# Rounding the angles of the tables in one VectorE step, own space for the first projection, and a new written-out order, in an attention and spectral-gate kernel on one core

## The chip, the cores and the metric

One core of one Trainium2 chip runs the whole program. The metric is the device time of one execution in microseconds, the lower the better; the time of the kernel before is the median of three runs.

## The reference, cut to what matters

There are 8 batches, 8 heads, 576 positions and 64 dimensions of a head. The first half is an attention with feature maps, the second a gate with a convolution over the sequence, done by Fourier tables.

```python
def phi(x):
    proj = np.einsum('bhsd,df->bhsf', x, w_phi)             # 64 -> 128 features
    proj = proj - np.max(np.abs(proj), axis=-1, keepdims=True)
    return np.concatenate([np.exp(proj), np.exp(-proj)], axis=-1)
q_p, k_p = phi(q), phi(k)
kv = np.einsum('bhsf,bhsd->bhfd', k_p, v)
z = np.sum(k_p, axis=2)
num = np.einsum('bhsf,bhfd->bhsd', q_p, kv)
den = np.einsum('bhsf,bhf->bhs', q_p, z)[..., None] + 1e-06
x = num / den                                               # then as [batch, 576, 512]
x1, x2, x3 = split(x @ w_proj)                              # 512 -> 3 * 512
x2_conv = irfft(rfft(x2, axis=1) * rfft(filter_fft, axis=0), axis=1)
out = (x1 * x2_conv * x3) @ w_out
```

All inputs and the output are float32; the matmuls take bf16.

## The kernel before

**Order.** The whole program is one list of words, `PLAN` (lines 26 to 184). `run` (L995 on) takes the words from first to last and calls the method of that name with the arguments behind it; `@n` is the PSUM bank that the word uses, and `ACT`, `DVE` or `POOL` the engine that does a copy or an elementwise step. Each engine, and each DMA queue, therefore does its instructions in the order in which their words stand, and an instruction that waits holds up all that stands behind it on its engine. Waits between engines are set from the tiles that instructions read and write. Buffers are rings (`RING`): `kn`, `qn`, `vn`, `kT` and `qT` have two each, one for even and one for odd batches.

**Loads.** `load,n,b` (L560) brings batch `b` of q, k or v from HBM to SBUF as bf16, 576 KB written, on GpSimd's (POOL's) queue; `loadh` (L566) half a batch, 288 KB; `w_load,proj,i` (L550) a third of the projection weights, 512 KB; `w_load,out` (L553) the output weights. All of them are issued by POOL, in the order of the list and between POOL's own arithmetic.

**Transposes.** The features need q and k with dimensions along partitions. Batch 0 is transposed on TensorE (`pt`, L582) and copied out of PSUM (`pte`). The other batches go by DMA transposes on SyncE's (SP's) queue: `trh,n,b,X` (L572), one for heads 0 to 3 (X = 0) and one for heads 4 to 7 (X = 1), 288 KB each. SP also issues the filter loads (L481, L485), the transposes of the attention's output (`trx` L786, `trxt` L791) and the stores of the result (`st` L994).

**Attention, for each batch.** `Pk` (L601) and `Qn` (L608) multiply k and q with `w_phi`, four words each; `Pkt` and `Qnt` (L616) do the ninth block of positions of all heads at once, so each of these two needs both halves of the transposed batch. `maxk`, `maxq` and their `t` forms (L677) are the maxima of absolute values on VectorE (DVE), `ex` (L663) the exponentials on ScalarE (ACT), `vs` (L719) scales v on POOL, `KV` (L734) sums keys times values, `Pq` (L635, L641) is the projection of q with its maximum taken off, `NE` (L748) the numerator and denominator, `rc` (L762) and `xn` (L767) the division.

**Gate, for each batch.** `f1` (L816) and `f2` (L822) fold the positions by sums and differences, `F` (L828, L832) is the Fourier transform with the tables `D` and `Dt`, `X1`, `X2`, `X3` are the projections (L872 and L850; `X1t`, `X3t` L881 for the last 64 positions), `X1e` copies the first projection to the tile `x1s`, `tm` (L913) multiplies the third into it, `Y1` (L860) multiplies the spectrum with the filter's, `m3` (L864) adds two products, `I` (L925) is the inverse transform with the table `inv` (`J`, L963, for the last batch), `Ip` and `Im` (L932) give `cv`, `ym` (L973) multiplies by `x1s`, `O` (L984) is the output projection, `Oe` its copy out of PSUM, `st` the store.

**Tables, once at the start.** POOL writes rows of numbers (`gen_rows`), DVE makes columns of factors (`gen_cols`, L364 on). An angle in turns is row times column plus a phase: ACT computes it (`gen_turns`, L424 and L428) into the tile `turn`; DVE rounds it to a whole number by a cast to int32 (L437) and subtracts that (L438, `gen_angles`); ACT takes the sine (`gen_sin`). `H` (L511) and `H_ev` are the filter's own transform. What is needed at the start alone lies in a scratch pool; `late` closes it and puts `T0` to `T4`, `x1s`, `es`, `cv`, `yT` and `o` in its place, so their first writes wait for the last readers of the scratch tiles.

Of the kernel before, what the change touches and what calls it, by code (L numbers as in the profile page):

```python
# [32 lines left out]
pte,DVE,k,0,0,0@6 gen_sin,0 trh,q,1,0 maxq,0,3@4 gen_back pte,ACT,q,0,0,1@0 Pk,0,1@6 Pk,0,0@2
gen_sin,2 Qnt,0@0 load,q,2 maxk,0,0@2 Qn,0,0@4 gen_sin,4 load,v,1 maxqt,0@0 filt_fold,POOL,0
ex,k,p,0,1@6 maxq,0,0@4 D1m@0 D1e,DVE@0 pt,k,0,1,0@4 pt,k,0,1,1@5 gen_ends,POOL pte,DVE,k,0,1,0@4
Qn,0,1@0 pte,ACT,k,0,1,1@5 ex,k,m,0,0@2 gen_five,DVE H,0@5 load,k,2 gen_neg maxk,0,1@6
filt_fold,POOL,1 ex,k,p,0,0@2 maxq,0,1@0 ex,k,m,0,1@6 Pk,0,2@2 maxk,0,2@2 mhi,0 Pkt,0@0 Pk,0,3@6
H_ev,ACT,0@5 mlo,POOL,0 H,4@4 maxkt,0@0 ex,k,m,0,2@2 H,3@5 maxk,0,3@6 em,p,0,0 exkt,p,0@0
vs,POOL,p,0,0 trh,k,1,0 H_ev,DVE,3@5 ex,k,p,0,2@2 ex,k,m,0,3@6 trm,0@2 H,2@3 H_ev,DVE,4@4 em,m,0,0
H,1@5 trme,DVE,0@2 em,p,0,1 exkt,m,0@0 vs,POOL,m,0,0 H_ev,DVE,2@3 ex,k,p,0,3@6 Pqt,0@0 H_ev,DVE,1@5  # L40
late Pq,0,1@2 exqt,m,0@0 Qn,1,3@6 exqt,p,0@0 vs,POOL,p,0,1 ex,q,p,0,1@2 maxq,1,3@6 KV,0,0@0
ex,q,m,0,1@2 trh,k,1,1 Pq,0,2@4 KVe,DVE,0,0@0 Qn,1,2@6 em,m,0,1 load,q,3 ex,q,p,0,2@4 Qnt,1@2
maxq,1,2@6 Qn,1,0@0 vs,POOL,m,0,1 ex,q,m,0,2@4 maxq,1,0@0 Pq,0,0@6 Qn,1,1@4 ex,q,p,0,0@6 maxqt,1@2
NE,0,1@0 load,v,2 maxq,1,1@4 ex,q,m,0,0@6 KV,0,1@2 rc,0,1@0 mhi,1 xn,0,1@0 NE,0,0@4 mlo,POOL,1
KVe,ACT,0,1@2 trm,1@6 rc,0,0@4 ptx,0,1@0 trme,ACT,1@6 xn,0,0@4 NEt,0@2 ptxe,ACT,0,1@0 NE,0,2@6
f1,POOL,0,0,0 rct,0@2 ptx,0,0@4 xnt,0,0@2 Pq,0,3@0 ptxe,ACT,0,0@4 rc,0,2@6 xnt,0,1@2 xn,0,2@6
f1,POOL,0,0,1 ex,q,p,0,3@0 ptxt,0@2 trh,q,2,0 Pqt,1@4 ptxte,DVE,0@2 ptx,0,2@6 ex,q,m,0,3@0 Pk,1,1@2
f2,POOL,0,0,0 ptxe,DVE,0,2@6 X1t,0@7 trh,q,2,1 maxk,1,1@2 exqt,m,1@4 NE,0,3@0 f2,POOL,0,0,1
X1te,ACT,0@7 X3t,0@6 exqt,p,1@4 rc,0,3@0 ex,k,p,1,1@2 xn,0,3@0 load,k,3 Pkt,1@4 tmt,0@6 ptx,0,3@0
ex,k,m,1,1@2 f1,POOL,0,1,1 maxkt,1@4 F,0,1@6 ptxe,DVE,0,3@0 Fet,ACT,0,1@6 f1,POOL,0,1,0 Pk,1,0@2  # L50
Fe,ACT,0,1@6 Pk,1,3@0 maxk,1,0@2 exkt,p,1@4 X1,0,2@6 exkt,m,1@4 f2,POOL,0,1,1 ex,k,p,1,3@0 X1,0,1@7
trh,k,2,0 X1e,DVE,0,2@6 f2,POOL,0,1,0 ex,k,p,1,0@2 X1,0,3@4 maxk,1,3@0 trh,k,2,1 ex,k,m,1,0@2
X1,0,0@6 load,q,4 X1e,DVE,0,3@4 X3,0,3@5 em,p,1,0 X1e,DVE,0,1@7 ex,k,m,1,3@0 vs,POOL,p,1,0
X1e,DVE,0,0@6 F,0,3@2 em,m,1,0 trh,k,3,0 tm,0,3@5 X3,0,0@0 Fet,ACT,0,3@2 Fe,ACT,0,3@2 F,0,2@4
vs,POOL,m,1,0 tm,0,0@0 X3,0,1@3 Fet,ACT,0,2@4 Fe,ACT,0,2@4 F,0,0@0 tm,0,1@3 Qnt,2@4 Pk,1,2@6
Fet,ACT,0,0@0 load,k,4 Fe,ACT,0,0@0 maxqt,2@4 Pkt,2@2 trh,k,3,1 ex,k,m,1,2@6 maxkt,2@2 X2,0,0@0
ex,k,p,1,2@6 X2,0,4@4 Y1,0,0@0 exkt,m,2@2 X2,0,1@5 exkt,p,2@2 maxk,1,2@6 Qn,2,1@0 KV,1,0@2 Y1,0,4@4
em,m,1,1 em,p,1,1 vs,POOL,m,1,1 Pq,1,1@6 maxq,2,1@0 KVe,ACT,1,0@2 X3,0,2@4 ex,q,p,1,1@6 Y1,0,1@5
Qn,2,2@0 ex,q,m,1,1@6 Pq,1,2@2 vs,POOL,p,1,1 tm,0,2@4 X2,0,2@5 ex,q,m,1,2@2 maxq,2,2@0 Pk,2,1@6
ex,q,p,1,2@2 X2,0,3@4 Y1,0,2@5 load,k,5 ex,k,p,2,1@6 NE,1,1@0 m3,POOL,0,0 Y1,0,3@4 Pq,1,0@2  # L60
ex,k,m,2,1@6 trh,q,3,0 rc,1,1@0 ex,q,m,1,0@2 maxk,2,1@6 Qn,2,3@4 m3,POOL,0,1 ex,q,p,1,0@2 maxq,2,3@4
Qn,2,0@6 NE,1,0@2 maxq,2,0@6 Pq,1,3@4 load,v,3 ex,q,m,1,3@4 trh,q,3,1 rc,1,0@2 xn,1,1@0 I,0,0@6
ex,q,p,1,3@4 xn,1,0@2 I,0,1@0 f1,DVE,1,0,1 trx,1,0 Ie,0,0@6 KV,1,1@2 f1,POOL,1,0,0 Ie,0,1@0 Im,0,0@6
mhi,2 Ip,0,0@6 Im,0,1@0 Pk,2,2@4 ym,POOL,0,0 Pk,2,3@6 Ip,0,1@0 KVe,ACT,1,1@2 maxk,2,2@4 ex,k,p,2,3@6
NEt,1@2 ym,POOL,0,1 NE,1,2@0 ex,k,m,2,3@6 rct,1@2 xnt,1,0@2 rc,1,2@0 trx,1,1 mlo,POOL,2 xnt,1,1@2
ex,k,p,2,2@4 f2,DVE,1,0,0 load,q,5 NE,1,3@2 maxk,2,3@6 ex,k,m,2,2@4 trxt,1 f2,POOL,1,0,1 rc,1,3@2
# [983 lines left out]
```

## Time and profile before

| | |
|---|---|
| runs | 340.84, 340.9 and 342.14 us, median 340.9 |
| the profiled execution's own time | 341.41 us |
| its span, first to last instruction | 339.6 us |
| mean granted TensorE clock | 0.975 |
| TensorE (PE) busy | 283.2 us, 83% |
| VectorE (DVE) busy | 269.4 us, 79% |
| ScalarE (ACT) busy | 225.3 us, 66% |
| GpSimd (POOL) busy | 217.3 us, 64% |
| DMA moved | 39.98 MB, 118 GB/s on average |

The profile is of one execution. 1.8 us of its time lie outside its span. Busy shares are averages over the whole span: the start is unlike the middle, so stretches are read one by one. TensorE's clock is given as a share of 2.4 GHz: 1.00 is that level and 0.50 is 1.2 GHz. Names such as `kn_78` in the rows of the order are tiles: `kn_77` and `kn_78` are the two buffers of `kn`, for even and odd batches, `qn_75` and `qn_76` those of `qn`, `vn_79` and `vn_80` those of `vn`.

### The profile page before, as it was taken

The numbers are of one execution on the slowest core, as the hardware profiler recorded it, in microseconds if no ns is written. First come the engines' busy times: TensorE is split into PE (matmuls) and PEld (weight loads), VectorE is DVE, ScalarE is ACT, GpSimd is POOL, SyncE is SP. The second block draws the span as 40 slices with busy tenths as digits, with TensorE's granted clock in tenths as the row PEclk, the third lists the DMA queues.
The fourth block names the chain that finished last, engine by engine and source line by source line (L and its number), as shares of the span: only waits on it lengthen the run. The fifth ranks groups of instructions, "written<-read, shape, count | busy, mean of one in ns | idle before, by whom it ended". The sixth has DMA issues, their size and how long they took to land.

```text
span 339.6 us, 10233 instructions
## 1 busy us (share of the span) xinstructions
PE 283.2 (83%) x4289; PEld 202.8 (60%) x4289; DVE 269.4 (79%) x450; ACT 225.3 (66%) x376; POOL 217.3 (64%) x186
## 2 busy tenths in 40 slices
PE   0566785887698997897999898999999899989992
...
GB/s 122 247 194 181 200 168 188 163 173 119 145 145 181 120 86 64 223 75 146 105 94 196 106 70 128 137 5 141 126 70 2 28 135 7 36 71 131 26 0 154
DMA packets 72030, 39.98 MB, mean 118 GB/s; under 512 B 52336, under 2 KB 66800, under 8 KB 71984
## 3 DMA queue, kind: packets, MB, share of 16 engines
...
q14 instruction: 13, 0.11, 0.1%
HBM read 33.75 MB, written 9.44 MB: 127 GB/s over the span
## 4 chain that ended last, share of the span: by engine, by line
PE 53%; DMA 21%; DVE 9%; POOL 6%; issue 4%; ACT 4%; SPq 1%; ACTq 0%; DVEq 0%; POOLq 0%
PE ps L872 13%; DMA kT<-kn 10%; PE ps L850 9%; DMA kn<-in_k_dram 7%; PE ps L984 6%; PE ps L925 5%; PE ps L734 4%; DMA out_dram<-o 2%; PE ps L828 2%; PE ps L748 2%; PE ps L832 2%; PE ps L881 2%; DVE xn L767 2%; DVE cv L932 2%; DMA xT<-xn 2%
## 5 line engine op out<-in xcount | busy, mean ns | idle before, releaser
L872 PE MATMUL ps<-xT,wproj 128*128 128x256 bf16 x512 | 64.7, 276 | 2.5 <-DMA xT<-xn 1.7
L973 POOL TENSOR_TENSOR yT<-cv,x1s 128x576 bf16<-128x576 f32 x27 | 34.1, 1277 | 37.1 <-DVE x1s L913 16.9
L872 PEld LDWEIGHTS <-wproj 128*128 128x128 bf16 x512 | 48.6, 99 | 12.1 <-issue 3.3
L677 DVE TENSOR_REDUCE mk<-ps 128x8 f32<-128x1024 f32 (+1 forms) x40 | 44.0, 1109 | 8.8 <-PE ps L616 6.4
L677 DVE TENSOR_REDUCE mq<-ps 128x8 f32<-128x1024 f32 (+1 forms) x40 | 43.6, 1109 | 8.5 <-PE ps L608 5.8
L719 POOL TENSOR_TENSOR vp<-vn,vp 128x1152 bf16<-128x1152 bf16 x16 | 35.8, 2235 | 8.7 <-ACT vp L713 8.5
L663 ACT ACTIVATE Eqp<-ps 128x1024 bf16<-128x1024 f32 x32 | 32.3, 1032 | 10.4 <-PE ps L641 10.4
L663 ACT ACTIVATE Eqm<-ps 128x1024 bf16<-128x1024 f32 x32 | 32.4, 1031 | 6.9 <-PE ps L641 6.9
L663 ACT ACTIVATE Ekm<-ps 128x1024 bf16<-128x1024 f32 x32 | 32.8, 1031 | 5.9 <-PE ps L601 3.0
L663 ACT ACTIVATE Ekp<-ps 128x1024 bf16<-128x1024 f32 x32 | 32.7, 1030 | 5.2 <-PE ps L601 5.2
L864 POOL TENSOR_TENSOR T<-T,T 128x1024 bf16<-128x1024 bf16 x12 | 25.3, 2126 | 16.4 <-DVE T L860 16.4
L984 PE MATMUL ps<-wout,yT 128*128 128x512 bf16 x144 | 33.5, 379 | 2.5 <-DVE yT L967 0.8
L281 ACT COPY o<-ps 128x512 f32<-128x512 f32 x35 | 20.4, 589 | 22.5 <-PE ps L984 17.1
L719 POOL TENSOR_TENSOR vm<-vn,vm 128x1152 bf16<-128x1152 bf16 x14 | 30.1, 2152 | 7.3 <-ACT vm L713 7.3
L816 POOL TENSOR_TENSOR SD<-xn 128x512 bf16<-128x512 bf16 x26 | 29.7, 1161 | 5.2 <-DVE xn L767 5.1
L850 PE MATMUL ps<-wproj,XF 128*128 128x512 bf16 x128 | 31.5, 388 | 0.0
L925 PE MATMUL ps<-inv,T 128*128 128x288 bf16 x168 | 25.6, 295 | 3.7 <-POOL T L864 1.9
L932 DVE TENSOR_TENSOR cv<-es,ps 128x288 f32<-128x288 f32 x56 | 22.5, 446 | 6.5 <-ACT es L929 5.8
L822 POOL TENSOR_TENSOR xf<-SD 128x512 bf16<-128x512 bf16 x24 | 27.3, 1158 | 0.4
L913 DVE TENSOR_TENSOR x1s<-ps,x1s 128x512 bf16<-128x512 f32 x32 | 21.7, 685 | 3.0 <-PE ps L872 2.4
L984 PEld LDWEIGHTS <-yT 128*128 128x128 bf16 x144 | 13.4, 98 | 17.3 <-issue 1.4
L860 DVE TENSOR_TENSOR T<-ps,HTo 128x1024 bf16<-128x1024 f32 x16 | 19.3, 1218 | 4.6 <-PE ps L850 4.3
(174 smaller groups left out, 676.5 us busy)
## 6 DMA issues: line engine op xcount, KB each, us to landing
...
```

The costliest lines, as they stand in the source:

```text
L663: self.nc.scalar.activation(e, p, AF.Exp, bias=0.0, scale=1.0 if g == "p" else -1.0)
L677: self.nc.vector.tensor_reduce(out=out, in_=src, axis=AX.X, op=ALU.max, apply_absolute_value=True)
L719: self.eng(eng).tensor_tensor(out=t[:, :, :, 0:64], in0=self.at("vn", b)[:, 2 * X:2 * X + 2], in1=t[:, :, :, 64:65].to_broadcast([128, 2, ...
L816: self.eng(eng).tensor_tensor(out=o[:, :, 2 * i:2 * i + 2, :], in0=x[:, :, 0:2, :], in1=x[:, :, 2:4, :], op=ALU.subtract if i else ALU.add)
L822: self.eng(eng).tensor_tensor(out=o[:, :, 2 * i:2 * i + 2, :], in0=x[:, :, 0:4:2, :], in1=x[:, :, 1:4:2, :], op=ALU.subtract if i else ALU ...
L850: self.mm(self.pb(0), l, w[:, kt, 512:1024], start=(kt == 0), stop=(kt == 3))
L864: self.eng(eng).tensor_tensor(out=Y, in0=Y, in1=self.at(f"T{2 * e + 1}", b), op=ALU.add)
L872: self.mm(o[:, d], w[:, kt, f0 + 128 * m:f0 + 128 * m + 128], y[:, 1, ::-1, ::-1] if d else y[:, 0], start=(kt == 0), stop=(kt == 3))
L925: self.mm(self.pb(e, 0, 288), l, inv[:, 2 * e + i if i < 2 else 4 + e, :], start=(i == 0), stop=(i == 2))
L932: self.nc.vector.tensor_tensor(out=self.at("cv", 4 * b + m)[:, :, odd, :], in0=self.at("es", 4 * b + m).rearrange("p (x t) -> p x t", t=32 ...
L973: self.eng(eng).tensor_tensor(out=self.at("yT", b)[:, m, 0:SEQ], in0=self.at("cv", 4 * b + m).rearrange("p x h t -> p (x h t)"), in1=self. ...
L984: self.mm(self.pb(0), y[:, kt, 128 * c:128 * c + 128], w[:, kt, :], start=(kt == 0), stop=(kt == 3))
```

## The change

**Angles.** `gen_turns` is gone. DVE computes row times column plus phase straight into an int16 tile (a `tensor_scalar` whose result is rounded by the type of its output), and one `scalar_tensor_tensor` gives row times column minus that whole number. The phase is added as the bias of the sine on ACT; the sines are split accordingly (two for `D`, four for `Dt`, two and two for `inv[0:4]`, two as before for the last). `gen_cols` is cut in two words and `gen_rows` in two, and three pairs of iota instructions become one each.

**Space.** `x1s` moves from the tiles that follow the scratch pool to the ones that stand from the start.

**Order.** Every line of `PLAN` is new. Words change engine in a few places: 8 of the 36 copies `Oe` go from ACT to DVE, 11 of the 32 `X1e` from DVE to ACT, 6 `Fe` and 3 `Fet` from ACT to DVE, 4 `pte` from ACT to DVE, and 2 `vs`, 1 `ym` and 3 `m3` from DVE to POOL, 3 `f1` from POOL to DVE.

```diff
-TWO_PI = 2.0 * math.pi
+TWO_PI = 6.283185
 PLAN = """
-zeros gen_rows w_load,phi filt_load,2 w_phi loadh,q,0,0 filt_loadt gen_cols loadh,q,0,1 filt_load,0
-load,q,1 loadh,k,0,0 filt_load,1 w_load,proj,0 filt_fold,DVE,2 gen_turns,2 loadh,k,0,1 gen_turns,4
...
+w_load,phi filt_load,2 filt_load,0 filt_load,3 filt_loadt filt_load,1 loadh,k,0,0 gen_part
+loadh,k,0,1 gen_ident gen_rows,0 loadh,q,0,0 zeros pt,k,0,0,1@0 pte,ACT,k,0,0,1@0 gen_cols,0
...
     def alloc(self):
...
         R("XFt", [128, 4, 128], BF16)
+        R("x1s", [128, 4, SEQ], BF16)
     def late(self):
...
         R("T4", [128, 512], BF16)
-        R("x1s", [128, 4, SEQ], BF16)
...
-    def gen_turns(self, i):
...
-            for sine in range(2):
-                a.activation(t[:, :, sine, :], self.fr[:, :, sine, :], AF.Identity,
-                             bias=col(8 if sine else 23), scale=col(i))
...
-    def gen_angles(self, eng, i):
-        e, r = self.eng(eng), self.span(i)
-        t, w = self.turn[:, r, :], self.whole[:, r, :]
-        e.tensor_copy(w, t)
-        e.tensor_tensor(out=t, in0=t, in1=w, op=ALU.subtract)
+    def gen_angles(self, i):
...
+        def rest(k, a, b, x):
+            v.scalar_tensor_tensor(out=self.turn[:, a:b].rearrange("p a x -> p (a x)"), in0=x,
+                                   scalar=col(k), in1=self.whole[:, a:b].rearrange(
+                                       "p a x -> p (a x)"), op0=ALU.mult, op1=ALU.subtract)
+        if i in (0, 2):
+            w = self.whole[:, i:i + 2].rearrange("p o (s f) -> p o s f", s=2)
+            for sine in range(2):
+                v.tensor_scalar(out=w[:, :, sine, :], in0=self.fr[:, :, sine, :], scalar1=col(i),
+                                scalar2=0.0 if sine else 0.25, op0=ALU.mult, op1=ALU.add)
+            rest(i, i, i + 2, self.fr.rearrange("p o s f -> p (o s f)"))
+            return
+        for k in ((3, 4), (5, 6, 7))[i - 3]:
+            v.tensor_scalar(out=self.whole[:, 1 + k], in0=self.nr, scalar1=col(k),
+                            scalar2=col(8 + k), op0=ALU.mult, op1=ALU.add)
+            rest(k, 1 + k, 2 + k, self.nr)
     def gen_sin(self, i):
...
-            a.activation(self.at("D"), t, AF.Sin, **kw)
...
+        def sin(o, x, bias, scale=TWO_PI):
+            a.activation(o, x, AF.Sin, bias=bias, scale=scale)
...
-        self.whole = s.tile([128, 9, 288], I32, name="whole")
+        self.whole = s.tile([128, 9, 288], I16, name="whole")
```

**The loads on POOL's queue, at the start of the program.** Before, q and k of batch 0 come with q of batch 1 between them, and behind `kn_78` (k of batch 1) five more loads stand ahead of the first `vs` (`vp_104`):

```order
L566 DMA qn_75<-in_q_dram 128x2x576 x2
L560 DMA qn_76<-in_q_dram 128x4x576
...
L560 DMA vn_79<-in_v_dram 128x4x576
L560 DMA kn_78<-in_k_dram 128x4x576
L553 DMA wout_67<-in_moe_w_out_dram 128x4x512
L550 DMA wproj_66<-in_moe_w_proj_dram 128x4x512
...
L560 DMA qn_75<-in_q_dram 128x4x576
L560 DMA vn_80<-in_v_dram 128x4x576
...
L560 DMA kn_77<-in_k_dram 128x4x576
...
L719 TENSOR_TENSOR vp_104<-vn_79,vp_104 128x18x64
```

After the change the same place reads:

```order
L577 DMA qn_76<-in_q_dram 128x4x576
L567 DMA wproj_66<-in_moe_w_proj_dram 128x4x512
...
L577 DMA kn_78<-in_k_dram 128x4x576
L577 DMA kn_77<-in_k_dram 128x4x576
L510 TENSOR_TENSOR fe<-fl 128x1024 x2
L736 TENSOR_TENSOR vp_104<-vn_79,vp_104 128x18x64
L718 TENSOR_TENSOR mh_89<-mq_87,mh_89 128x2x18
L736 TENSOR_TENSOR vm_119<-vn_79,vm_119 128x18x64
L736 TENSOR_TENSOR vp_105<-vn_79,vp_105 128x18x64
L736 TENSOR_TENSOR vm_118<-vn_79,vm_118 128x18x64
L567 DMA wproj_66<-in_moe_w_proj_dram 128x4x512
L577 DMA qn_75<-in_q_dram 128x4x576
```

k of batches 1 and 2 are now the last loads for a while: the second third of the projection weights, q of batch 2, v of batch 1 and the output weights moved behind batch 0's four `vs`.

**The transposes on SP's queue.** Before, and after, the first ones behind the filter loads are:

```order
L572 DMA_TRANSPOSE qT_82<-qn_76 128x9x128 x2
L572 DMA_TRANSPOSE kT_84<-kn_78 128x9x128 x2
L572 DMA_TRANSPOSE qT_81<-qn_75 128x9x128 x2
L572 DMA_TRANSPOSE kT_83<-kn_77 128x9x128 x2
L572 DMA_TRANSPOSE kT_84<-kn_78 128x9x128 x2
```

```order
L589 DMA_TRANSPOSE qT_82<-qn_76 128x9x128 x2
L589 DMA_TRANSPOSE kT_84<-kn_78 128x9x128 x2
L589 DMA_TRANSPOSE kT_83<-kn_77 128x9x128 x2
L589 DMA_TRANSPOSE qT_81<-qn_75 128x9x128 x2
L589 DMA_TRANSPOSE kT_84<-kn_78 128x9x128 x2
```

Batch 1 keeps its place (q, then k); of batch 2, k goes ahead of q, and within a pair the second half of k now goes first.

**ACT, from its first instruction to the sines of the last tables.** In the change:

```order
L281 ACT_TABLE_LOAD
L281 COPY kT_83<-ps 128x512
L458 ACT_TABLE_LOAD
...
L680 ACT_TABLE_LOAD
L680 ACTIVATE Ekm_108<-ps 128x1024
...
L458 ACT_TABLE_LOAD
L458 ACTIVATE inv_70<-turn,cols_74 128x288 x4
...
L680 ACT_TABLE_LOAD
L680 ACTIVATE Ekm_110<-ps 128x1024
...
L458 ACT_TABLE_LOAD
L458 ACTIVATE inv_70<-turn,cols_74 128x288 x2
L680 ACT_TABLE_LOAD
```

Before there were three such loads, for the turns (L424), the sines (L452) and the exponentials (L663); now there are seven, since two groups of sines stand between exponentials.

## Rows read from the trace of the kernel before

**Rows 1.** The page: busy time, the span in 40 slices.
```profile
PE 283.2 (83%) x4289; PEld 202.8 (60%) x4289; DVE 269.4 (79%) x450; ACT 225.3 (66%) x376; POOL 217.3 (64%) x186
...
PE   0566785887698997897999898999999899989992
```

**Rows 2.** Windows: start:end, length, busy PE PEld DVE ACT POOL, clock, DMA, GB/s.
```profile
0.00:10.30 10.30, 1.30 (x11) 1.14 (x12) 3.82 (x40) 3.60 (x6) 9.56 (x27) 1.00 0.74 146
10.30:43.40 33.10, 21.12 (x343) 13.73 (x340) 31.68 (x48) 29.83 (x47) 23.05 (x24) 1.00 1.22 198
43.40:57.20 13.80, 9.00 (x174) 7.14 (x174) 7.63 (x17) 7.92 (x15) 6.90 (x8) 0.83 1.26 180
57.20:85.30 28.10, 23.21 (x312) 16.05 (x311) 21.10 (x25) 18.87 (x30) 18.95 (x13) 0.90 1.10 158
85.30:121.80 36.50, 31.61 (x527) 22.93 (x527) 30.29 (x47) 23.64 (x41) 18.73 (x15) 0.95 0.90 142
121.80:160.70 38.90, 33.52 (x526) 24.19 (x523) 34.58 (x51) 25.26 (x42) 27.21 (x20) 1.00 0.69 120
160.70:195.30 34.60, 32.47 (x523) 23.38 (x523) 29.20 (x45) 23.78 (x41) 28.46 (x21) 1.00 0.72 127
...
333.10:339.60 6.50, 0.00 (x0) 0.00 (x0) 0.00 (x0) 1.07 (x2) 0.00 (x0) 0.72 0.64 148
```

**Rows 3.** Chain of waits that ended last, 0 to 62 us: start, us, what.
```profile
9.41 22.56 DMA kn<-in_k_dram
31.98 1.75 SPq L572
33.78 20.71 DMA kT<-kn
```

**Rows 4.** PE's timeline: the two waits for transposed k of batches 1 and 2.
```profile
54.54 0.29 PE L616 MATMUL ps<-wphi,kT 64*128 64x128 bf16 x2 [3.46 <-DMA kT<-kn]
...
69.51 0.23 PE L616 MATMUL ps<-wphi,kT 64*128 64x128 bf16 x2 [2.36 <-DMA kT<-kn]
```

**Rows 5.** DVE's timeline: the last division of batch 0 ahead of X1.
```profile
49.94 0.69 DVE L767 TENSOR_TENSOR xn<-ps,r 128x512 bf16<-128x512 f32 x1
```

**Rows 6.** DMA queues (packets, MB, share): POOL's queue q0, 4 to 36 us.
```profile
q0 software_dynamic: 4599, 4.87, 92.2%
```

**Rows 7.** The same, SP's queue q1, 28 to 32, then 64 to 68 us.
```profile
q1 hardware_dynamic: 565, 0.14, 27.1%
...
q1 hardware_dynamic: 2589, 0.65, 125.9%
```

**Rows 8.** Timeline of all engines at the start: where ACT and DVE begin the tables.
```profile
6.68 1.28 ACT L424 ACT_TABLE_LOAD   x1 [6.68 <-DVE cols L416]
...
9.78 0.63 DVE L491 CAST f<-flt 64x512 bf16<-64x512 f32 x1 [2.80 <-DMA flt<-in_moe_filter_fft_dram]
...
10.34 0.43 DVE L437 CAST whole<-turn 128x576 int32<-128x576 f32 x1
```

**Rows 9.** Groups by line and form: the angles on ACT, and on DVE.
```profile
L428 ACT ACTIVATE turn<-nr,cols 128x288 f32<-128x288 f32 x5 | 2.8, 611 | 0.0
L424 ACT ACTIVATE turn<-fr,cols 128x288 f32<-128x288 f32 x4 | 2.3, 615 | 0.0
...
L438 DVE TENSOR_TENSOR turn<-turn,whole 128x576 f32<-128x576 f32 x3 | 2.3, 758 | 0.1
L437 DVE CAST whole<-turn 128x576 int32<-128x576 f32 x3 | 1.4, 467 | 0.0
```

**Rows 10.** ACT's timeline around its third table load.
```profile
19.76 0.95 ACT L456 ACTIVATE inv<-turn,cols 128x288 bf16<-128x288 f32 x2
20.73 1.28 ACT L663 ACT_TABLE_LOAD   x1
...
22.03 1.02 ACT L663 ACTIVATE Ekp<-ps 128x1024 bf16<-128x1024 f32 x1
```

**Rows 11.** Chain of waits, 150 to 170 us: start, us, what.
```profile
156.40 4.21 POOL T L864 x2
...
162.31 0.50 PE ps L748 x16
162.81 0.21 PE ps L635 x2
...
169.59 0.40 PE ps L608 x8
```

**Rows 12.** Groups by form: a maximum, and m3's sum on DVE.
```profile
L677 DVE TENSOR_REDUCE mq<-ps 128x8 f32<-128x1024 f32 x32 | 38.6, 1215 | 6.2 <-PE ps L608 5.8 <-ACT Ekm L663 0.4
...
L864 DVE TENSOR_TENSOR T<-T,T 128x1024 bf16<-128x1024 bf16 x4 | 2.8, 690 | 0.1
```

More of the change, by code (lines that the diff above doesn't have):

```diff
@@ L11 @@
 I32 = mybir.dt.int32
+I16 = mybir.dt.int16
 AF = mybir.ActivationFunctionType
@@ L33 @@
[L33 to L66, printed above, removed]
-em,m,2,1 I,0,2@6 xn,1,3@2 em,p,2,1 vs,POOL,m,2,1 xn,1,2@0 F,1,1@4 Ie,0,2@6 I,0,3@2 trx,1,2 Im,0,2@6
```

398 lines of the change are left out of this document (219 added, 179 removed).

## The prediction

> **What bounds the kernel now.** I read the page first. Over the whole span TensorE is busy 83% and VectorE 79% of the time [rows 1], so neither is idle enough for one edit to matter everywhere; but the slices show PE at half load or less in the first tenth and again around a sixth of the span, and near nine tenths after that. So I cut the span at events of the program: 10.3 us (DVE's first rounding), 43.4 (the first division of batch 0), 57.2 (the first X1 of batch 0), 85.3 (the first I of batch 0), then the first I of batches 1, 2 and 3, and 333.1, the end of the last matmul [rows 2]. To be seen there: from 10.3 to 43.4 DVE is busy 31.7 of 33.1 us, so DVE sets the pace. From 43.4 to 57.2 nothing is full: PE works 9.0 of 13.8 us, DVE 7.6. From 57.2 to 85.3 PE is idle 4.9 us and its clock averages 0.90. From 85.3 on PE sets the pace: of 247.8 us up to 333.1 it works 283.2 less the 54.6 of the first four stretches, 228.6 us, and idles 19.2, of which 4.9 and 5.4 lie in the first two stretches and 2.1 in the third.
>
> Why is the piece from 43 to 57 empty? The chain of waits says: k of batch 1 is issued at 9.4 us, lands 22.6 us later, and its transposes take another 20.7 us, until 54.5 [rows 3]. PE, in order, reaches Pkt of batch 1 before any X1 of batch 0 and waits 3.46 us for it; the same happens at 69.5 with Pkt of batch 2, 2.36 us [rows 4]. The last division of batch 0 ends at 50.6 [rows 5]; with a transpose and a copy X1 could have begun near 51.5, not 57.2.
>
> Why do transposes take so long? While POOL's queue is full of loads, it moves 4.87 MB in 32 us, 0.152 MB per us [rows 6], and SP's queue gets 0.14 MB in 4 us; when the loads pause, SP's queue moves 0.65 MB in 4 us [rows 7]. A half batch of k is 128 x 1152 bf16, 0.295 MB: 8.4 us beside loads, 1.8 us without.
>
> **The change, part by part: up to the first X1.**
> - *Loads.* Ahead of k of batch 1 stand the same bytes as before, so it lands near 30 us as now. What follows differs: k of batch 2 is the last load (six of 0.59 and two of 0.52 MB by then, 4.58 MB, at 0.152 MB per us from 2.4 us: landed near 32.5), and the next load waits on POOL behind batch 0's four vs, the first of which needs exponentials of maxima. I put it at 37 to 39 us. In the pause of some 5 us the transposes in the queue (half of q1, both halves of k1) need 3 x 1.8 us: k1 is ready near 39 instead of 54.5, and PE asks for it near 45. This wait goes. What is late next is DVE.
> - *Angles and DVE.* DVE idles before 9.8 for the filter's last rows and gets ACT's first turns at 10.3, since ACT starts with a table load at 6.7 [rows 8]. In the change DVE needs only its columns and POOL's rows, by some 6 us; so its work starts 4.3 us sooner, and I give 2 us back for q and k that have not landed. ACT loses 2.8 + 2.3 us of turns. DVE's rounding now is 0.758 (subtraction) + 0.467 (cast) for 576 columns [rows 9]. The two new forms are in no row: from below the same, from above two passes at 0.758 per 576. Nearest is 0.758 for the form with two tensors and a cast's price split in two: 1.36, and with the nine pieces 6.2 us against 5.3, bounds 5.2 and 7.9. DVE also gets four copies of batch 0 (some 0.45 each) and gives away two copies of the filter, four of D and one maximum; by my count of its words up to the first X1 it has 1.1 us more. So X1 begins near 51.5 + 1.1 - 4.3 + 2 = 50 us, **7.2 us sooner**; bounds 47 (nothing given back, rounding as now) and 52.
> - *ACT's table loads.* Four more, 1.28 us each [rows 10]. They lie in two pairs with sines between: 2 x 1.28 + four sines of half a us + a sign change, some 5.3 us, beside four maxima of q and one of k at 1.215 us on DVE [rows 12], 6.1; and 2 x 1.28 + two sines, 3.5 us, beside a copy, two maxima and a division, also 3.5. I take nothing for them; uncovered they cost 5.1. The row shows a whole switch, from the end of the sine at 20.71 to the start of the exponential at 22.03, in 1.32 us. *The Trainium skill, "ScalarE: Activation LUTs", section "What ACT_TABLE_LOAD costs", counts a drain of about 1.38 us on top, 2.66 us a switch; by that the second pair would stick out by some 2.8 us and the total by as much; the trace has no such drain.*
> - *Own space for x1s.* In the trace the first write to it (X1te, near 49 us) waits for PE, never for scratch tiles. Nothing; it would cover a late scratch reader if X1 came 10 us sooner still.
>
> **From the first X1 to the first I.** Before: 28.1 us with DVE busy 21.1. By words, DVE has 2.7 us less to do here now (two maxima, two X1e and a division fewer, a copy more): 18.4. Half of its 7.0 idle us belong to the wait at 69.5 and the low clock behind it; I leave 3.6. So 22.0 us, **6.1 less**; bounds 19 and 28.
>
> **Moved behind the first I.** Two NE (0.50), two Pq (0.21 + 3 x 0.11) and two Qn (0.40) now stand behind it [rows 11]: **+3.0 us** of PE work later on.
>
> **From the first I to the end.** The same PE work in another order. I cannot read a term per word from a trace of the old order. The two early stretches idle 4.9 and 5.4 us, partly the aftermath of the late start; if they fell to 2.1 each, 6 us would go. I take a third, **-2.0**; bounds -8 and +17 (every one of the seven stretches as bad as 5.4 is 37.8 against 19.2). The end after the last matmul, 6.5 us [rows 2], stays: the fifth copy still waits for a buffer of the first store.
>
> **Sum.** 339.6 - 7.2 - 6.1 + 3.0 - 2.0 = 327.3 us of span; with 1.8 outside it 329.1 against the profiled execution's own 341.4. That lies 0.5 above the median of 340.9, so **329 us** against the median. (Differences under 0.5%, 1.7 us, are about what these runs can't tell from none.)
>
> **Rivals.**
> 1. *The wait moves to q of batch 2.* Its load now comes second behind the pause (landed near 45), behind it five more (4.0 MB, to about 64 us). Its transposes then crawl at 8.4 us a half, behind those of k2: 64 us if k2 used the pause, 72 if not. PE asks for Qnt of batch 2 near 63. At worst 9 us, more than the gain of the second stretch: **335 us**. For it: the whole stretch from 10 to 57 shows this contention [rows 2, 7]. Against it: k2's halves are issued in the pause. Chance 0.19.
> 2. *k of batch 1 stays late.* If loads resume before the pause lets the queue empty (vs earlier than I think, or loads landing slower), four halves at 8.4 us from q1's landing near 22 end at 56, and the half that Pk of batch 1 needs is the fourth. X1 stays at 57, the work moved changes nothing: **341 us**, no change. Chance 0.12.
> 3. *The table loads lie open.* 5.1 us: **334 us**. Chance 0.06.
> 4. *Slower: POOL's sums hold up the inverse transform.* m3 takes 2.1 us on POOL and 0.69 on DVE [rows 11, 12]; the change gives POOL three more of them, two vs and a ym. Before batch 2's I, two of these sums (4.21 us) already end the chain at 160.6, in the worst stretch. If all seven stretches idled 5.4 us like this one, 18.6 us more would be lost, 8.3 net of the other terms: **349 us**. It decides once a stretch idles over 4.2 us. Against it: POOL is busy only 64% of the span [rows 1], and of the change's extra sums that of the last batch has X3's matmuls beside it. Chance 0.14.
>
> **How the numbers follow.** The forecast has 0.45, and 0.04 is left for more gain than its bounds. Faster: 0.45 + 0.19 + 0.06 + 0.04, and a little of the second rival, 0.77; same: most of that rival, 0.09; slower: 0.14. The forecast's own range is 318 to 336. To leave out no more than 2 in 10 it is drawn up over rivals 1 to 3 and the milder part of rival 4, to 344.
>
> **What would show it.** X1 of batch 0 near 50 us, with no wait of L616's counterpart for transposed k over 1 us: the first step. I of batch 0 near 72, and the clock at 1.00 between: the second. PE idle from there to the last matmul near 17 us: the third. Wrong if PE waits for q of batch 2 near 63 (rival 1), for k1 (rival 2), if DVE waits for the exponentials of batch 0 behind a table load (rival 3), or if I waits for POOL in most stretches (rival 4).

## The result, and the profile after

The changed kernel took **322.79 us** (median of four runs, 321.47 to 326.3), the kernel before beside it 341.52 us (four runs, 340.84 to 342.92). The ratio is **0.9434**, with a 95% interval of 0.9378 to 0.949. A median here is of all runs, while a ratio leaves out those that a lower clock lengthened (of the change, 326.3 us). The forecast was 329 us in a range of 318 to 344. The profiled execution took 323.44 us, 1.7 of it outside its span of 321.7; the granted clock averaged 0.994, after 0.975 before.

The page of the changed kernel, busy time and slices of the span (the answer to [rows 1]):

```profile
PE 272.9 (85%) x4263; PEld 199.7 (62%) x4289; DVE 272.0 (85%) x461; ACT 224.3 (70%) x374; POOL 227.1 (71%) x186
...
PE   1532887998999979979899978998999999998981
...
PEclk9999999999999999999999999999999999999997
```

The half-empty slices around a sixth of the span are gone, and no slice but the last, most of it behind the last matmul, shows a lower clock. The thin start is not gone: the third and fourth slices are emptier than before (3 and 2 for 6 and 6). (26 of 4289 matmul records are missing, so PE's idle time below is somewhat overstated.) Windows of the changed kernel, cut at the same events as [rows 2], with its columns: the first X1 of batch 0 comes at 54.4, its first I at 73.3, the first I of batches 1, 2 and 3 at 107.7, 141.3 and 177.1, and the last matmul ends at 315.1.

```profile
18.50:43.40 24.90, 13.22 (x264) 8.56 (x267) 24.34 (x28) 17.52 (x30) 15.25 (x11) 1.00 1.12 175
43.40:54.40 11.00, 7.90 (x162) 6.42 (x160) 10.52 (x22) 10.21 (x14) 5.91 (x7) 1.00 1.16 194
54.40:73.30 18.90, 18.51 (x278) 13.57 (x277) 17.69 (x23) 17.36 (x31) 17.81 (x15) 1.00 1.27 173
73.30:107.70 34.40, 32.77 (x629) 25.30 (x632) 29.32 (x50) 27.95 (x47) 29.30 (x21) 1.00 1.09 160
107.70:141.30 33.60, 31.64 (x480) 23.13 (x480) 28.50 (x45) 25.11 (x43) 26.61 (x20) 1.00 0.96 150
141.30:177.10 35.80, 31.21 (x515) 22.25 (x510) 30.11 (x46) 26.16 (x45) 23.79 (x17) 1.00 0.61 103
177.10:315.10 138.00, 130.68 (x1898) 95.27 (x1907) 115.61 (x188) 87.98 (x152) 92.38 (x65) 1.00 0.44 85
315.10:321.70 6.60, 0.03 (x1) 0.00 (x0) 0.69 (x1) 0.59 (x1) 0.00 (x0) 0.71 0.65 149
```

Three of these stretches carry the gain. From the first X1 to the first I it is 18.9 us instead of 28.1, PE busy 18.5 of them. The next two take 34.4 and 33.6 instead of 36.5 and 38.9. The first X1 itself came only 2.8 us sooner, and everything from the first I of batch 2, at 141.3 us, to the last matmul takes 173.8 instead of 172.4.

Why so little in the head? The timeline of the changed kernel, 18.5 to 26 us, shows one instruction:

```profile
18.53 6.98 DVE L448 TENSOR_SCALAR whole<-nr,cols 128x288 int16<-128x288 f32 x1
18.57 4.67 POOL L510 TENSOR_TENSOR fe<-fl 128x1024 bf16<-128x1024 f32 x2
...
23.18 2.15 POOL L736 TENSOR_TENSOR vp<-vn,vp 128x1152 bf16<-128x1152 bf16 x1
...
25.98 0.42 DVE L448 TENSOR_SCALAR whole<-nr,cols 128x288 int16<-128x288 f32 x1
```

A rounding that takes 0.42 us elsewhere lasted 6.98. It ended at 25.51, 0.18 us behind a run of three POOL instructions without a gap (18.57 to 25.33). On the PE timeline the maxima queued behind it became a wait of 8.32 us:

```profile
28.51 1.04 PE L625 MATMUL ps<-wphi,qT 64*128 64x128 bf16 x16 [8.32 <-DVE mq L694]
```

### The profile page after: what moved, and what is told of

The parts are those of the page before. It is cut to its first block, busy times and chain, and to the rows that moved or that the text cites. A ratio compares the mean times of both kernels' runs of the same rounds, so it can differ in the third digit from the quotient of the medians.

```text
span 321.7 us, 10206 instructions
## 1 busy us (share of the span) xinstructions
PE 272.9 (85%) x4263; PEld 199.7 (62%) x4289; DVE 272.0 (85%) x461; ACT 224.3 (70%) x374; POOL 227.1 (71%) x186
## 4 chain that ended last, share of the span: by engine, by line
PE 51%; DVE 22%; DMA 9%; ACT 8%; issue 5%; SPq 3%; POOL 1%; ACTq 0%; DVEq 0%
PE ps L889 15%; PE ps L867 9%; PE ps L751 4%; PE ps L942 4%; DVE mq L694 4%; DMA out_dram<-o 3%; PE ps L1001 3%; PE ps L765 3%; DVE mk L694 3%; DVE xn L784 3%; DVE whole L448 2%; DVE T L877 2%; PE ps L849 2%; PE ps L845 2%; PE ps L652 2%
## 5 line engine op out<-in xcount | busy, mean ns | idle before, releaser
L889 PE MATMUL ps<-xT,wproj 128*128 128x256 bf16 x512 | 63.2, 273 | 1.2 <-DVE x1s L930 0.8
L990 POOL TENSOR_TENSOR yT<-cv,x1s 128x576 bf16<-128x576 f32 x28 | 35.5, 1282 | 20.7 <-DVE cv L949 14.0
L881 POOL TENSOR_TENSOR T<-T,T 128x1024 bf16<-128x1024 bf16 x15 | 31.7, 2124 | 15.1 <-DVE T L877 15.0
L736 POOL TENSOR_TENSOR vm<-vn,vm 128x1152 bf16<-128x1152 bf16 x16 | 34.4, 2155 | 10.9 <-ACT vm L730 9.8
L736 POOL TENSOR_TENSOR vp<-vn,vp 128x1152 bf16<-128x1152 bf16 x16 | 34.4, 2151 | 6.6 <-ACT vp L730 3.1
L680 ACT ACTIVATE Eqp<-ps 128x1024 bf16<-128x1024 f32 x32 | 32.6, 1027 | 7.5 <-PE ps L658 7.3
L1001 PE MATMUL ps<-wout,yT 128*128 128x512 bf16 x134 | 33.4, 379 | 4.0 <-ACT o L281 1.9
L833 POOL TENSOR_TENSOR SD<-xn 128x512 bf16<-128x512 bf16 x23 | 26.6, 1171 | 6.4 <-DVE xn L784 6.2
L867 PE MATMUL ps<-wproj,XF 128*128 128x512 bf16 x118 | 30.1, 380 | 0.5
L281 ACT COPY o<-ps 128x512 f32<-128x512 f32 x27 | 15.6, 595 | 18.2 <-PE ps L1001 12.0
L281 ACT CAST x1s<-ps 128x512 bf16<-128x512 f32 (+1 forms) x31 | 16.7, 551 | 13.1 <-PE ps L889 12.1
L942 PE MATMUL ps<-inv,T 128*128 128x288 bf16 x168 | 24.0, 286 | 2.0 <-issue 1.9
```

Of the source, the lines that this page charges most:

```text
L281: self.nc.scalar.copy(dst, src)
L680: self.nc.scalar.activation(e, p, AF.Exp, bias=0.0, scale=1.0 if g == "p" else -1.0)
L736: self.eng(eng).tensor_tensor(out=t[:, :, :, 0:64], in0=self.at("vn", b)[:, 2 * X:2 * X + 2], in1=t[:, :, :, 64:65].to_broadcast([128, 2, ...
L833: self.eng(eng).tensor_tensor(out=o[:, :, 2 * i:2 * i + 2, :], in0=x[:, :, 0:2, :], in1=x[:, :, 2:4, :], op=ALU.subtract if i else ALU.add)
L867: self.mm(self.pb(0), l, w[:, kt, 512:1024], start=(kt == 0), stop=(kt == 3))
L881: self.eng(eng).tensor_tensor(out=Y, in0=Y, in1=self.at(f"T{2 * e + 1}", b), op=ALU.add)
```

## The experiments

All ratios are to the kernel before, run beside each kernel; 322.8 us, the change, stands at 0.9434. Where the profile is of an execution over 2 us off the median of its runs, that is said. The table gives what the runs are read by, in us, from times before rounding: the first X1 of batch 0, the stretch from there to the first I of batch 0, the next two from first I to first I, and from the first I of batch 2 to the end of the last matmul.

| kernel | median, ratio (95%) | first X1 | X1 to I | I,0 to I,1 | I,1 to I,2 | rest |
|---|---|---|---|---|---|---|
| before | | 57.2 | 28.1 | 36.5 | 38.9 | 172.4 |
| the change | 322.8, 0.943 (0.938 to 0.949) | 54.4 | 18.8 | 34.4 | 33.7 | 173.8 |
| old_order | 342.8, 1.001 (0.996 to 1.005) | 58.5 | 26.5 | 38.0 | 38.0 | 171.9 |
| old_angles | 326.2, 0.963 (0.943 to 0.982) | 55.9 | 18.8 | 34.4 | 33.1 | 173.3 |
| late_loads2 | 340.9, 1.004 (0.991 to 1.016) | 54.1 | 29.2 | 36.4 | 39.6 | 173.9 |
| early_loads | 328.2, 0.961 (0.956 to 0.967) | 58.0 | 18.8 | 34.4 | 33.0 | 175.3 |
| angles_early | 322.9, 0.948 (0.939 to 0.956) | 55.0 | 18.8 | 34.4 | 32.6 | 173.6 |
| angles_late | 330.8, 0.980 (0.964 to 0.995) | 61.0 | 19.2 | 34.4 | 33.2 | 173.4 |
| open_pause | 332.8, 0.984 (0.967 to 1.001) | 50.8 | 33.2 | 34.4 | 32.6 | 173.7 |
| new_then_old | 340.0, 1.000 (0.992 to 1.009) | 55.6 | 24.6 | 41.3 | 41.6 | 172.3 |
| old_then_new | 338.8, 0.998 (0.991 to 1.006) | 59.1 | 31.4 | 34.4 | 32.6 | 176.0 |
| sines_early | 320.9, 0.940 (0.932 to 0.947) | 53.2 | 18.9 | 34.5 | 32.6 | 174.7 |

### Which part of the change: old_order and old_angles

```diff
-zeros gen_rows w_load,phi ... gen_cols ... gen_turns,2 ... gen_angles,DVE,2
+zeros gen_part gen_rows,0 gen_rows,1 w_load,phi ... gen_cols,0 gen_cols,1 ... gen_angles,2
```

> The order of before with the other two parts of the change in it: the angles rounded in one VectorE step (no turns on ScalarE) and own space for x1s. Theory (the new order makes the gain): the wait for the transposed k of batch 1 still sets the first X1 of batch 0, within 1.5 us of 57.2, and the time is 339 to 343 us. Rival (the shorter way to the angles makes the gain): first X1 at 53 or sooner, time 333 us or less.

342.8 us, ratio 1.0005 (0.9962 to 1.0049): the new angles and x1s's own space together are worth nothing in the old order. **The gain is the order.** (The order includes the engines of its words. The list ahead of the prediction gives net counts of some kinds; word by word, 101 of the 344 that name an engine have another one. No run separates this from the places of the words.) The other way round, the old angles in the new order:

```diff
+... gen_turns,0 gen_angles,0 ... gen_turns,2 gen_angles,2 ... gen_turns,4 gen_angles,4 ... gen_turns,3 gen_angles,3
     def gen_angles(self, i):
-        v.tensor_scalar(...)
-        v.scalar_tensor_tensor(...)
+        v.tensor_copy(w, t)
+        v.tensor_tensor(out=t, in0=t, in1=w, op=ALU.subtract)
```

> The changed kernel with the angles computed as before (turns on ScalarE ahead of each rounding, cast and subtraction on VectorE, phase inside the turn), x1s and the order as in the change. Theory (the order makes the gain, the angles a little of it): ScalarE has 5.1 us more work in the first 45 us and VectorE waits for it at the first rounding, first X1 of batch 0 at 55 to 57 us instead of 54.4, time 323 to 326 us. Rival (the short way to the angles is what makes the new head possible): time 330 us or more.

326.2 us, 3.4 more than the change in the median; its interval overlaps that of the change, so the angles are not told from nothing here either (the profiled execution, at 323.8, is 2.4 under its median). X1s's own space was not taken back by itself in the new order. X1 at 55.9 was as expected. The hole in VectorE's work stays, with another cause: now it waits 5.26 us for ScalarE's turns, and the cast behind them is short.

```profile
26.04 0.61 DVE L452 CAST whole<-turn 128x864 int16<-128x864 f32 x1 [5.26 <-ACT turn L443]
```

### The pause in the loads: late_loads, late_loads2, early_loads

```diff
-... H,0 load,k,2 gen_neg ...
+... load,k,1 load,k,2 ... pt,k,0,0,1 ... vs,POOL,m,0,1 w_load,proj,1 load,q,2 load,v,1 w_load,out ...
```

> The kernel before with one thing of the new order: k of batch 2 is loaded right behind k of batch 1, the four loads that stood behind it (last third of the projection weights, output weights, q of batch 2, v of batch 1) go behind the scaling of v of batch 0, and the transposes of k of batch 2 ahead of those of q. Theory (the pause in the loads makes the transposes of k fast): the waits of 3.46 and 2.36 us for transposed k fall under 0.5 us each, the first X1 of batch 0 comes at 52 to 54 us instead of 57.2, the granted clock from there to the first I is 1.00 instead of 0.90, and the time is 331 to 336 us. Rival (the wait moves to q of batch 2, whose load is now late): first X1 early, but a wait of over 3 us for transposed q before the first I, time 337 to 342 us.

357.4 us, ratio 1.046, and this says nothing of the pause: I had put the load of k of batch 2 ahead of batch 0's transposes on TensorE, and the two share a buffer, so that k of batch 0 was replaced by that of batch 2 and PE waited 19.6 us for the load. The next kernel leaves that load in place:

```diff
-... w_load,out ... w_load,proj,1 ... load,q,2 ... load,v,1 ...
+... vs,POOL,m,0,1 w_load,proj,1 load,q,2 load,v,1 w_load,out ...
+... trh,k,1,1 trh,k,2,0 trh,k,2,1 ...
```

> The kernel before with the four loads (last third of the projection weights, output weights, q and v of the batches behind) moved behind the scaling of v of batch 0, the load of k of batch 2 left where it stood (behind the last reader of batch 0's k), and k of batch 2 transposed ahead of q of batch 2. Theory (the pause in the loads makes the transposes fast): waits of TensorE for transposed k under 0.5 us each (3.46 and 2.36 us before), first X1 of batch 0 at 52 to 54 us instead of 57.2, time 331 to 336 us. Rival (the wait moves to q of batch 2, which is loaded late): first X1 early, but over 3 us of waiting for transposed q before the first I, time 337 to 342 us.

X1 came at 54.1, 3.2 us sooner, and PE waited for no transposed k; but the rival is what happened, 340.9 us. PE's timeline:

```profile
65.14 0.29 PE L616 MATMUL ps<-wphi,qT 64*128 64x128 bf16 x2 [3.31 <-DMA qT<-qn]
```

The wait moved to q of batch 2, X1 to I grew by 1.1 us, and by the first I of batch 4 nothing of the 3.2 us was left (230.8 against 231.1 before). Now the same four loads without the pause, in the new order:

```diff
-... xn,0,1 ... f1,DVE,0,0,0 w_load,proj,1 load,q,2 load,v,1 w_load,out ...
+... vs,POOL,p,0,0 w_load,proj,1 load,q,2 load,v,1 w_load,out ...
```

> The changed kernel with those four loads issued as soon as the first scaling of v is done (near 25 us instead of 41 to 44 us), so that the queue has no pause. Theory: transposes of batch 1 take over 15 us in all instead of about 8, TensorE waits over 2 us for transposed k or q of batch 1, first X1 of batch 0 at 57 us or later (54.4 in the changed kernel), time 326 to 332 us. Rival (the new order asks for k of batch 1 late enough anyway): first X1 within 1 us of 54.4, time 321 to 324 us.

328.2 us and X1 at 58.0, as the theory had it (the wait for transposed q of batch 1 was 1.92 us, just under the 2 it named). The queues in the window from 36 to 40 us, first of the change, then of early_loads (packets, MB, share):

```profile
q1 hardware_dynamic: 3595, 0.90, 112.3%
```

```profile
q0 software_dynamic: 583, 0.65, 93.5%
q1 hardware_dynamic: 585, 0.14, 27.5%
```

Alone, the transposes' queue moves 0.90 MB in 4 us; beside loads 0.14. The 3.5 us by which X1 came later stayed lost to the end (first I of batch 2 at 144.2 against 141.3, last matmul 4.4 us later). So in the new order the pause is worth about 5 us; in the old one, nothing.

### The long rounding: angles_early, angles_early2, angles_late

```diff
-... filt_fold,POOL,2 gen_rows,1 ... gen_five,DVE maxk,0,2 ... gen_angles,4 maxqt,0 ...
+... gen_rows,1 filt_fold,POOL,2 ... gen_five,DVE gen_angles,4 maxk,0,2 ... maxqt,0 ...
```

> The changed kernel with the row of positions made earlier on GpSimd (ahead of a cast) and the rounding of the last three angles of the first group moved on VectorE ahead of a maximum and two copies, so that it is over before GpSimd's two filter sums begin. Theory (VectorE's rounding was held up 6.5 us by GpSimd's run of sums over SBUF): all three roundings take 0.4 to 0.9 us, the first X1 of batch 0 comes at 48 to 50 us instead of 54.4, time 316 to 319 us. Rival 1 (the 6.98 us are something else, such as a wait for the row): one rounding is still over 3 us. Rival 2 (another engine sets X1 as well): roundings short, but X1 within 1.5 us of 54.4 and the time 321 to 324 us.

322.9 us, no change, because the long instruction was only moved. VectorE and GpSimd in this kernel:

```profile
16.85 0.61 DVE L448 TENSOR_SCALAR whole<-nr,cols 128x288 int16<-128x288 f32 x1
...
17.93 5.01 DVE L448 TENSOR_SCALAR whole<-nr,cols 128x288 int16<-128x288 f32 x1
...
18.09 4.67 POOL L510 TENSOR_TENSOR fe<-fl 128x1024 bf16<-128x1024 f32 x2
```

Two roundings of the same row were short and the third, which meets the filter sums, lasted until 22.94, 0.18 us behind the end of GpSimd's run at 22.76: the same 0.18 as before. Rival 1 (a wait for the row) is out. Next, 5 us ahead of the sums:

```diff
+... gen_rows,1 gen_back ... maxk,0,1 maxk,0,0 gen_angles,4 ...
```

> The changed kernel with the row of positions made at 10 to 11 us on GpSimd and the three roundings moved on VectorE behind the second maximum (near 13 us), 5 us ahead of GpSimd's filter sums. The previous try moved them to 15.3 to 23.0 us and its third rounding still began 0.16 us ahead of the sums and ended 0.2 us behind them. Theory (held up by GpSimd's run of sums): all three roundings now take under 0.9 us, the wait of 8 us in TensorE's head is gone, first X1 of batch 0 at 48 to 50 us, time 316 to 319 us. Rival (something else sets X1 as well): all three short, X1 at 53 us or later, time 321 to 324 us.

All three took 0.42 to 0.50 us and the wait of 8 us was gone, which settles that GpSimd's run was the cause. The time did not move: 325.3 us (322.4 to 328.2, ratio 0.924 to 0.985; its profile is of the longest of these, so its stages are not compared). Where the gain went is asked of a third variant:

```diff
-... gen_angles,4 ... gen_sin,4 gen_neg ... gen_angles,3 ... gen_sin,3 ...
+... KVe,DVE,0,0 gen_angles,3 gen_angles,4 ... gen_sin,3 gen_sin,4 gen_neg late ...
```

> The changed kernel with the last three roundings moved on VectorE from 18.5 us to behind the copy of batch 0's second KV, next to the two that stood near there (GpSimd has then done its scalings of v), and all sines of inv in one group on ScalarE ahead of the end of the scratch space: two table loads fewer (2.6 us of ScalarE). Theory: no rounding over 0.9 us, ScalarE's 5.3 us of loads and sines no longer lie before the exponentials of q, 2.8 us of rounding come back later in the head: first X1 of batch 0 at 46 to 50 us, time 314 to 319 us. Rival (the sines are now late and hold up the inverse transform, or GpSimd's sums hold up the roundings there too): first I of batch 0 still at 72 us or later, time 321 us or more.

330.8 us, 8 more than the change, and X1 at 61.0. Its late loads and transposes, POOL's and SP's timelines:

```profile
33.65 0.81 POOL L567 DMA_DIRECT2D wproj<-in_moe_w_proj_dram  x1
```

```profile
23.73 7.71 SPq L589 DMA_TRANSPOSE qT<-qn  x2
31.55 17.83 SPq L589 DMA_TRANSPOSE kT<-kn  x4
```

The same two lines of the change:

```profile
41.48 0.81 POOL L567 DMA_DIRECT2D wproj<-in_moe_w_proj_dram  x1
```

```profile
24.09 7.59 SPq L589 DMA_TRANSPOSE qT<-qn  x2
31.78 8.06 SPq L589 DMA_TRANSPOSE kT<-kn  x4
```

The late loads stand on POOL behind the scalings of v, which wait for VectorE's maxima. With the hole gone they start at 33.65 instead of 41.48 and close the pause: the four transposes of k are issued over 17.8 us instead of 8.1 (in angles_early2, with late loads from 36.3 us, over 11.0). **The long rounding had been holding the pause open.** That the closed pause is what cost the time is not shown. TensorE waits for no transposed k ahead of X1 in angles_late. Its two longest waits from 20 us to X1 are for transposed q of batch 1, which landed at 33.7 us, sooner than in the change (35.6), and one in the middle of a group of matmuls for which the profile names no engine (4.0 us in angles_early2):

```profile
PE ps L625 <- DMA qT<-qn: 4.0, 1, 4.0
PE ps L765 <- issue: 3.1, 1, 3.1
```

The chain of waits to X1 runs through what the edit put there: five roundings from 41.2 to 45.2 us, and on ScalarE a table load, the sines and another load from 50.85 to 57.0:

```profile
50.85 1.28 ACT L458
52.14 1.87 ACT inv L458 x5
```

So the 6.6 us by which X1 was later than in the change belong at least in part to the moved sines and roundings; the share of each was not separated.

### The two halves of the order: new_then_old and old_then_new

```diff
-... (new order) I,0,0 ... (new order)
+... (new order) tm,0,2 ex,k,p,2,1 ... (what is left, order of before)
```

> The changed kernel up to the first I of batch 0 (with the two words that empty PSUM there), and all words that are left in the order of the kernel before. Theory (the part behind the first I gains by its own new order): the first I comes near 77 us (the 3 us of matmuls that the change moved behind it stand ahead of it again), from there to the last matmul it takes 242 to 247 us as before, and the time is 328 to 333 us. Rival (the part behind the first I is only quicker because it starts earlier and at full clock): 236 to 239 us from the first I on, time 321 to 325 us.

340.0 us, and neither theory nor rival named this: the first I comes at 80.2 us (77 was expected), and what is left of the head's gain is lost behind the seam. The two stretches take 41.3 and 41.6 us, longer than in any other kernel (the profiled execution took 343.8). Windows of the first, and its chain of waits:

```profile
80.20:121.50 41.30, 33.98 (x526) 24.21 (x526) 30.21 (x47) 23.90 (x41) 20.07 (x17) 0.88 0.90 149
```

```profile
86.15 9.83 DMA xTt<-xnt
```

Transposes of batch 1's result stand behind those of batch 3's k and q on SP's queue, as the old order has them, and now meet the loads; PE's clock falls to 0.88 of full.

```diff
-... (order of before) I,0,0 ... (order of before)
+... (order of before) ex,q,p,1,3 xn,1,0 ... (what is left, new order)
```

> The order of before up to the first I of batch 0, then all words that are left in the new order (angles and x1s as in the change). Theory (the part behind the first I gains by its own new order): first I near 85 us, 238 to 242 us from there to the last matmul, time 331 to 336 us. Rival (it gains only by its earlier start): 245 us or more behind the first I, time 339 to 343 us.

338.8 us, between the theory's 331 to 336 and the rival's 339 to 343; the 243.0 us from the first I to the last matmul lie between theirs too. Yet the two stretches behind the seam took 34.4 and 32.6 us, just as in the change:

```profile
90.42:124.80 34.38, 31.36 (x559) 23.34 (x559) 25.41 (x45) 24.28 (x42) 25.26 (x17) 0.96 0.71 111
124.80:157.40 32.60, 31.91 (x485) 23.20 (x483) 28.48 (x45) 25.02 (x43) 26.58 (x20) 1.00 0.83 149
```

Its first I came at 90.4, 5.4 us later than in old_order, with the same words on TensorE ahead of it (the profiled execution, at 341.7, is 2.9 over its median). From X1 on, its 312 matmuls took 25.1 us at a clock of 0.83, the 313 of old_order 22.1 at 0.93, and it waited 4.5 us for transposed k and q instead of 2.3; what set this off is left open. So the two shorter stretches belong to the order behind the first I, whatever the start, and the order ahead of it keeps its gain only before a continuation that fits.

### A version without the long rounding: open_pause and sines_early

```diff
+... gen_rows,1 gen_back ... maxk,0,0 gen_angles,4 ... D1e,ACT gen_sin,4 gen_neg ...
-... load,k,1 load,k,2 trh,k,1,1 trh,k,1,0 trh,k,2,1 trh,k,2,0 ...
+... load,k,1 trh,k,1,1 trh,k,1,0 ... load,k,2 trh,k,2,1 trh,k,2,0 w_load,proj,1 load,q,2 ...
```

> The changed kernel with the three roundings behind the second maximum as in angles_early2, their sines and the sign change right behind the first sines on ScalarE (one pair of table loads fewer), and k of batch 2 loaded behind the scaling of v, first of the late loads, so that the pause for the transposes of batch 1 begins one load sooner. Theory (taking the long rounding away let the late loads start 5 to 8 us sooner and collide with the transposes of batch 1; with the pause open at its front the gain comes through): transposed q and k of batch 1 are there by 35 us, no wait of TensorE over 1.5 us for them, first X1 of batch 0 at 47 to 51 us, time 314 to 319 us. Rival (the wait moves on to k or q of batch 2, now late): first X1 as early, but over 3 us of waiting for transposed k or q of batch 2 before the first I, time 320 to 324 us.

X1 at 50.8, as the theory said and as the prediction had it; time 332.8, worse even than its rival. PE's timeline:

```profile
70.95 0.29 PE L633 MATMUL ps<-wphi,qT 64*128 64x128 bf16 x2 [7.38 <-DMA qT<-qn]
76.47 0.29 PE L633 MATMUL ps<-wphi,qT 64*128 64x128 bf16 x2 [5.24 <-DMA qT<-qn]
```

k of batch 2 missed the pause, its transposes and those of q behind it ran beside loads, and X1 to I took 33.2 us. The last kernel is this one with the loads and transposes of batch 2 where the change has them:

```diff
-... load,k,1 trh,k,1,1 trh,k,1,0 ... load,k,2 trh,k,2,1 trh,k,2,0 w_load,proj,1 ...
+... load,k,1 load,k,2 trh,k,1,1 trh,k,1,0 trh,k,2,1 trh,k,2,0 ... w_load,proj,1 ...
```

> The changed kernel with the three roundings behind the second maximum and their sines and the sign change right behind the first sines on ScalarE (one pair of table loads fewer), all loads where the change has them. Theory (k of batch 2 loaded early uses the pause, ScalarE's loads and sines no longer lie ahead of the exponentials of q, the late loads start at 36 to 38 us when most of the six halves are transposed): no rounding over 0.9 us, first X1 of batch 0 at 50 to 53 us, no wait over 2 us for transposed q or k of batches 1 and 2, time 317 to 320 us. Rival (as with angles_early2 the sooner late loads take the gain back): X1 as early or not, a wait of over 2 us for transposed q or k, time 321 to 325 us.

320.9 us in six runs (318.2 to 323.2), ratio 0.9396 (0.9319 to 0.9473): as fast as the change, not told apart from it. The long rounding and a pair of table loads are gone, no transposed operand is waited for over 2 us, and X1 comes 1.2 us sooner. The late loads start at 37.7 us, 3.8 sooner than in the change, and the four transposes of k are issued over 6.8 us, so the pause was still long enough. Windows around it:

```profile
44.00:50.00 6.00, 3.83 (x75) 2.93 (x70) 5.85 (x14) 5.17 (x8) 3.65 (x4) 0.99 1.21 207
50.00:56.00 6.00, 6.00 (x67) 5.14 (x65) 4.34 (x9) 4.84 (x8) 5.29 (x6) 0.73 1.30 174
```

Just ahead of X1 the granted clock falls to 0.73, part of the window at the 1.2 GHz level, after PE had worked 3.8 of 6 us; in the change these six us had 1.00, with 3.65 us of work ahead. The slower matmuls there give back part of the 6.5 us; the rest was not followed.

## Why the prediction was right, and where it was not

Faster, and by more than the forecast: 322.8 for 329, inside its range. The span fell by 17.9 us where 12.3 were forecast; the terms were off on both sides: 4.4 us too much was promised up to the first X1 and 10.1 too little behind it. That the sum came out this near is in part these two set against each other. Of the signs it named, the first I came at 73.3 us (near 72), at a clock of 1.00, and PE idled 15.5 us from there to the last matmul (near 17); X1, at 54.4 instead of 50, missed.

- **Up to the first X1: forecast -7.2, measured -2.8.** The mechanism was there: late loads at 41.5 us (forecast 37 to 39), a pause in which the transposes ran at full rate, no wait for transposed k; early_loads shows its worth. The step that failed is the price of the angles. Nine pieces were to cost 6.2 us (5.2 to 7.9; the two passes at 0.758 us per 576 columns named as the upper bound make 6.8). By the groups they cost 7.7 us if the long one is counted at 0.42, and 6.6 more as it was. The bounds took a duration from rows without looking at what runs on GpSimd at that moment. The row was to be had: before, a pair of small copies, 0.25 us elsewhere, lasted 3.33 us at 23.22 beside a filter sum.

  The timeline of the kernel before:

```profile
23.22 3.33 DVE L472 COPY M<-D 128x64 bf16<-128x64 bf16 x2
23.25 0.79 POOL L560 DMA_DIRECT2D kn<-in_k_dram  x1
...
24.06 2.36 POOL L493 TENSOR_TENSOR fe<-fl 128x1024 bf16<-128x1024 f32 x1
...
26.55 0.25 DVE L472 COPY M<-D 128x64 bf16<-128x64 bf16 x2
```

  The Trainium skill, "SBUF — State Buffer", section "Who interferes with whom", names it: casts, copies and tensor_scalar can take the port pair that VectorE shares with GpSimd, and the one that is second stands still. The trace agrees that one stands still, and goes further: the wait lasted over three instructions of GpSimd in a row. Which was first it does not settle: VectorE's rounding is recorded as starting 0.04 us ahead of the run.
  And a second step fell with it: "what is late next is DVE" treated VectorE and the pause as two things. The pause ends when VectorE's maxima are done, so a sooner VectorE shortens it (angles_late, angles_early2). Nor was the price all that was in the way: sines_early has no long rounding, and its X1 comes at 53.2 us, not at 50.
- **First X1 to first I: forecast -6.1, measured -9.2.** Right in kind, a third too small. PE idles 0.4 us of it instead of 4.9; the other half of the gain is work, 18.5 us (278 matmuls at a clock of 1.00) instead of 23.2 (312 at 0.90). That it is the order of the words and not the absence of two waits is shown by the table: 18.8 to 19.2 us in six kernels with the new order on both sides of the first I, wherever X1 begins, and 29.2 in late_loads2, which has no wait for transposed k; 4.0 of these are waits for transposed q, which leaves 25. open_pause is the exception, and shows the price of a late load there.
- **Moved behind the first I, +3.0, and the rest, -2.0: forecast +1.0, measured -6.0.** The first two stretches gave 7.4 us, the rest cost 1.4. The step that failed is "I take a third": those two idled 10.3 us before and 3.6 after, so all that could be had by the prediction's own count was. And 0.95 of clock in the first stretch [rows 2] was read and not priced: the matmuls of the inverse transform in that stretch took 4.6 us before and 3.4 after (all 168 of the kernel 25.6 and 24.0). The upper bound of +17 is 18.6 by its own working, 37.8 less 19.2; nothing came near it. But the words "aftermath of the late start" were wrong: old_then_new starts late and has both stretches short, new_then_old starts early and has them long.
- **The table loads, priced at nothing.** A pair of them with its sines stood on the chain of waits from 30.9 to 36.1 us, because VectorE was late for them; sines_early, which takes a pair away together with the long rounding, gains nothing that can be measured. No sign of rival 3's 5 us in the change; in angles_late, where the sines of `inv` stand in one group later on, they lie on the chain for 6.1 us.
- **x1s, nothing, and the angles worth little by themselves:** right in the old order, by old_order; in the new one not told from nothing, by old_angles.
- **Rival 1** (q of batch 2) did not come in the change, but in late_loads2 and open_pause, where its load or the transposes ahead of it were moved. **Rival 2** did not come; early_loads, which fills the pause, brings back its late X1 (58.0) but not its 341 us. **Rival 4** did not come: PE's idle time behind POOL's sums ahead of I, 1.9 us before, is gone.
